# Fourier mixing and a gated FFN: the complex product summed on GpSimd, one inverse pass in place of two

## The chip, the cores and the metric

The kernel runs on one core of one Trainium2 chip. Its time is the device time of one execution in microseconds (us). Three runs of the kernel before took 885.06, 885.45 and 886.32 us, so the median is 885.45 us. The profile and the trace come from one further execution, which took 884.74 us.

A core has five engines, each with its own queue of instructions that it works through in order: TensorE (PE in the profile, with weight loads as PEld), VectorE (DVE), ScalarE (ACT), GpSimd (POOL) and SyncE (SP, which here only starts transfers). GpSimd starts transfers too. Engines wait for each other by semaphores. TensorE writes into PSUM, which has eight banks of 128 x 512 float32. ScalarE and VectorE read PSUM; in this kernel GpSimd works on SBUF alone.

## What is computed

```python
X = np.fft.rfft(x, axis=1)                       # x: (8, 3008, 256) float32
Y = X * (filt_r + 1j * filt_i)[None, :, :]       # filters: (1505, 256)
y = np.fft.irfft(Y, n=3008, axis=1)              # back to (8, 3008, 256)
t = y.reshape(24064, 256)
out = (np.maximum(t @ w_gate, 0.0) * (t @ w_val)) @ w_out   # widths 256 -> 1536 -> 256
```

The first three lines mix along the sequence of each of the 8 batches; the rest is a feed-forward part over all 24,064 tokens.

## The kernel before, in words

The sequence of 3008 is split as 94 x 32, and the transforms are done as matrix products. For each batch b there are five stages:

- A, the forward transform over 94. For batches 2 to 7 its input is loaded by `load_chunk` in four chunks j (six transfers each, started by GpSimd), folded by `fold_chunk` (six float32 additions and subtractions on GpSimd, L346 to L351), multiplied on TensorE in `tiled_a` (psF, L360), and stored to a buffer in device memory. `hold_gpsimd` (L259) puts a tiny copy on GpSimd in front of each load that waits for the newest `prod`, so that the load isn't started too early.
- `fwd(b, i)` for i = 0 to 5: the forward transform over 32, 16 matmuls of 64 x 32 weights into two banks psX (L396). The two halves r = 0 and 1 of the free dimension are the real and the imaginary part. The steps call it for two i at a time.
- `product(b, i, e, k)`: VectorE multiplies psX (both parts) by the real filter Ftr (k = 0, tile `tt`) or by the imaginary filter Fti (k = 1, tile `uu`), and writes bf16 (L413). `tt` and `uu` have four buffers each.
- `inv(b, q)` for q = 0 to 2: the inverse over 32. For each of two i and of two parts r there are two passes, k = 0 with the weights I2t over `tt`, and k = 1 with I2u over `uu`, and all four add up in PSUM: 64 matmuls of 32 x 64 weights and 256 columns into four banks psD (L428). I2u is I2t with its parts exchanged and signs changed, which does the complex arithmetic. ScalarE copies the four banks to `dsb` (L436), and SP stores it to device memory; `load_d` reads it back in another order.
- C, `item_c(k, h)`: the inverse over 94 for one block of 512 tokens (psY, L488), copied to `yT`, half h = 0 by ScalarE (L494) and half h = 1 by VectorE (L496).

The feed-forward part is the loop that everything else is hung into. The 24,064 tokens are 47 blocks k of 512, and each block has 12 steps. A step calls `gv` (four matmuls of 512 columns into psV and psG, a copy `vsb` on ScalarE, and on VectorE the `prod` of the gate and the value) and `o_part` of the block before (four matmuls of 256 columns into psO). After these two, the step calls the functions that were registered for it by `at_step`, in the order in which they were registered, and in steps 8 and 10 of a block `item_c` for the next block. There is no scheduler: this order is the order of every engine's queue. So a stage of a batch is put on TensorE by naming the global step, `k * 12 + ft`, at which it is called.

The steps are counted from `end`, a little before the batch's first output block. It is 51 for batch 1, and 123, 195, 267, 339, 411 and 483 for batches 2 to 7, 72 steps apart.

```python
l = (6, 14, 22, 30)[j] if b == 2 else end - 115 + NFT * j           # load of chunk j, then fold of chunk j - 1
l = (-37, -25, -13)[z] if b == 1 else -44 + 14 * z                  # start of fwd for pair z
at_step(end + l + (9 if b == 1 else 10) - (z == 2), lambda b=b, z=z: inv(b, z))
```

From `end + l` on, each of the 8 steps has one `product` (4 for the first i, 4 for the second), and `inv` follows behind them. The next batch's loads and folds are registered at steps of the present batch, for example those of batch 2 at steps 6 to 30, beside batch 1's products. In the prologue batch 0 runs alone, with 8 of its products on GpSimd (L411); it is not part of what is changed, except that its tables are shared.

Of the kernel before, what the change touches and what calls it, by code (L numbers as in the profile page):

```python
# [12 lines left out]
FP32 = mybir.dt.float32  # L13
BF16 = mybir.dt.bfloat16
ALU = mybir.AluOpType
# [16 lines left out]
NG = 24  # L32
# [3 lines left out]
def _ap(t, offset_elems, ap_list):  # L36
    return dataclasses.replace(
        t, offset=t.offset + offset_elems, ap=[list(p) for p in ap_list]
    )
# [77 lines left out]
def kernel(  # L117
# [10 lines left out]
    nc = tc.nc  # L128
    B, S_, D = x.shape
    DFF = moe_w_gate.shape[1]  # L130
    NFT = DFF // 128
# [11 lines left out]
    consts = ctx.enter_context(tc.tile_pool(name="consts", bufs=1))  # L143
# [5 lines left out]
    def bank(name, *shape):  # L149

        i = free.pop(0)
        t = ps.tile([128, *shape], FP32, tag=f"bank{i}", bufs=1, name=name)
        held[id(t)] = i, t
        return t

    def done(t):
        free.append(held.pop(id(t))[0])

    prologue = ExitStack()
    pro = prologue.enter_context(tc.tile_pool(name="pro", bufs=1))  # L160
# [12 lines left out]
    M1 = consts.tile([128, 2, N1], BF16)  # L173
    F2 = consts.tile([128, NG, 64], BF16)
    I2t = consts.tile([128, 2, NG // 2, 64], BF16)
    I2u = consts.tile([128, 2, NG // 2, 64], BF16)
    Ftr = consts.tile([128, NG // 2, D], BF16)
    Fti = consts.tile([128, NG // 2, D], BF16)
    WgT = consts.tile([128, 2, DFF], BF16)
# [17 lines left out]
    perm, conj, own = tabs[:, 0:64], tabs[:, 64:66], tabs[96:, 66:578]  # L197
# [94 lines left out]
    def turn_a(dst, src):  # L292

        nc.vector.transpose(dst.bitcast(FP32).rearrange("p k d -> p d k"),
                            src.bitcast(FP32).rearrange("p n d -> p d n"))
# [5 lines left out]
    def turn_1(i):  # L301
        w = D // 8
        src = AS1[1 + i // 2].rearrange("p l c d -> p (l c) d")
        turn_a(ats[1][:, 1, :, i * w:i * w + w], src[:, :, i % 2 * w:i % 2 * w + w])
# [36 lines left out]
    def fold_chunk(b, j):  # L341

        xp = XP[j]
        t = fs.tile([128, 2, 512], FP32, tag="fold", bufs=1, name="fold")
        tt = nc.gpsimd.tensor_tensor
        tt(t, xp[:, 0:2], xp[:, 2:4], op=ALU.add)  # L346
        tt(xp[:, 2:4], xp[:, 0:2], xp[:, 2:4], op=ALU.subtract)  # L347
        tt(xp[:, 1], xp[:, 2], xp[:, 3], op=ALU.add)
        tt(xp[:, 2], xp[:, 2], xp[:, 3], op=ALU.subtract)
        tt(xp[:, 0], t[:, 0], t[:, 1], op=ALU.add)  # L350
        tt(xp[:, 3], t[:, 0], t[:, 1], op=ALU.subtract)  # L351
        fold[b, j] = (xp[:, 0], xp[:, 3], xp[:, 1], xp[:, 2])

    def tiled_a(b, j):

        banks = [bank("psF", 2, D) for _ in range(4)]
        for c in range(4):
            for q in range(4):
                r = 32 * q
                nc.tensor.matmul(banks[q][32 * c:32 * c + 32], WF[r:r + 24, c, :],  # L360
                                 fold[b, j][c][r:r + 24], start=True, stop=True,
                                 tile_position=(r, 32 * c))
        asf = sb.tile([128, NC2 * D], BF16, tag="asb", bufs=3, name="asb")
        asf = asf.rearrange("p (n q d) -> p n q d", n=2, d=D)
        for q in range(4):
            copy = nc.scalar.copy if q % 2 == 0 else nc.vector.tensor_copy
            copy(asf[:, :, q, :], banks[q])  # L367
            done(banks[q])
        for c in range(4):
            nc.sync.dma_start(_ap(Abuf[b], ((48 * (c % 2) + 24 * (1 - c // 2)) * N2 + 8 * j) * D,  # L370
                                  [[N2 * D, 24], [1, 8 * D]]),
                              asf[32 * c:32 * c + 24])
# [12 lines left out]
    psXs, tus, left = {}, {}, {}  # L385
# [15 lines left out]
    def product(b, i, e, k, pool=False):  # L401

        psX = psXs[b, i, e]
        pool_, bufs = (fs, 4) if b else (pro, 8)
        p = pool_.tile([128, 2, D], BF16, tag=("tt", "uu")[k], bufs=bufs, name=("tt", "uu")[k])
        filt = (Ftr, Fti)[k][:, 2 * i + e, :]
        filt = dataclasses.replace(filt, ap=[list(filt.ap[0]), [0, 2], list(filt.ap[1])])
        if pool:
            xs = pro.tile([128, 2, D], FP32, tag="xs", bufs=3)
            nc.scalar.copy(xs, psX)  # L410
            nc.gpsimd.tensor_tensor(p, xs, filt, op=ALU.mult)  # L411
        else:
            nc.vector.tensor_tensor(p, psX, filt, op=ALU.mult)  # L413
        tus[b, i, e, k] = p
        left[b, i, e] -= 1
        if not left[b, i, e]:
            done(psX)

    def inv(b, q):

        psD = [bank("psD", 2, D) for c in range(4)]
        for m in range(2):
            for k in range(2):
                for r in range(2):
                    for c in range(4):
                        for e in range(2):
                            i = 2 * q + m
                            nc.tensor.matmul(psD[c][64 * e:64 * e + 64, m],  # L428
                                             (I2t, I2u)[k][32 * c:32 * c + 32, r, 2 * i + e, :],
                                             tus[b, i, e, k][32 * c:32 * c + 32, r],  # L430
                                             start=(k == r == 0), stop=(k == r == 1),
                                             tile_position=(32 * c, 64 * e))
        dst = sb.tile([128, 8, D], BF16, tag="dsb", bufs=3, name="dsb") if b else DS0[:, 8 * q:8 * q + 8, :]
        for c in range(4):
            copy = nc.vector.tensor_copy if not b and q == 2 and c < 2 else nc.scalar.copy
            copy(dst[:, c:8:4, :], psD[c])  # L436
            done(psD[c])
        if b:
            for z in range(4):
                nc.sync.dma_start(_ap(Dbuf[b], (64 * (z // 2) + z % 2) * NG * D + 8 * q * D,  # L440
                                      [[2 * NG * D, 32], [1, 8 * D]]),
                                  dst[32 * z:32 * z + 32])

    def first_b(amid):

# [36 lines left out]
    def item_c(k, h):  # L482

        if h == 0:
            yTs[k] = sb.tile([128, 2, W], BF16, tag="yT", bufs=3, name="yT")
        psY = bank("psY", W)
        for (o, b, n2, n1, w) in runs(k * W, W):
            nc.tensor.matmul(psY[:, o:o + w],  # L488
                             dCs[b, n2 // 8][:, n2 % 8, h * 128:(h + 1) * 128],
                             M1[:, 1, n1:n1 + w] if b == 0 else M1[:NROW, 0, n1:n1 + w],  # L490
                             start=True, stop=True)
        dst = yTs[k][:, h]
        if h == 0:
            nc.scalar.copy(dst, psY)  # L494
        else:
            nc.vector.tensor_copy(dst, psY)  # L496
        done(psY)
# [66 lines left out]
    q = NX2 * D // 4  # L564
# [54 lines left out]
    for p, s, h in items:  # L619
# [4 lines left out]
        if (p, s, h) == (3, 0, 1):  # L624
            for hh in range(2):
                item_c(0, hh)
    turn_1(0)
    nc.sync.dma_start(WF, nc.inline_tensor(fold_h, name="dft_fold").ap())
    prologue.close()
    fs = ctx.enter_context(tc.tile_pool(name="fs", bufs=2))  # L630
# [3 lines left out]
    def at_step(s, f):  # L634
        side.setdefault(s, []).append(f)
# [3 lines left out]
        at_step((4, 9, 12)[k - 1], lambda k=k: turn_1(k))  # L639
    for b in range(1, B):  # L640
        end = (b * S // W - 1) * NFT + C_AT[0] - 5
        if b > 1:
            for j, e in enumerate((-72, -67, -62, -57)):
                l = (6, 14, 22, 30)[j] if b == 2 else end - 115 + NFT * j

                def next_x(b=b, j=j, l=l):
                    hold_gpsimd(prods[-1][:, 0:8])
                    load_chunk(b, j)
                    if j:
                        fold_chunk(b, j - 1)  # L650
                    if j == 3:
                        fold_chunk(b, j)
                at_step(l, next_x)
                at_step(end + e, lambda b=b, j=j: tiled_a(b, j))
            at_step(end + e + 4, lambda b=b: load_at_tiled(b))
        for z in range(3):
            l = (-37, -25, -13)[z] if b == 1 else -44 + 14 * z
            for i in (2 * z, 2 * z + 1):
                at_step(end + l, lambda b=b, i=i: fwd(b, i))
                for h in range(4):  # L660
                    at_step(end + l + i % 2 * 4 + h, lambda b=b, i=i, h=h: product(b, i, h // 2, h % 2))
            at_step(end + l + (9 if b == 1 else 10) - (z == 2), lambda b=b, z=z: inv(b, z))
        at_step(end - 2, lambda b=b: load_d(b))
    prev = None
    for k in range(NB):
# [40 lines left out]
```

## Time and profile before

| | before |
|---|---|
| device time, median of 3 runs | 885.45 us |
| the profiled execution: device time | 884.74 us |
| the profiled execution: span of the instructions | 883.0 us |
| busy share PE / DVE / ACT / POOL | 98% / 65% / 56% / 41% |
| granted TensorE clock, mean | 1.00 |
| 564 copies `vsb` (ACT) | 592 ns each |
| 564 `prod` (DVE) | 690 ns each |
| products of L413 (DVE), 128x512 to bf16 | 681 to 683 ns each |
| 1536 matmuls of psD | 264 to 293 ns each, up to 8 of them at work side by side |
| GpSimd's additions, 128x1024 / 128x512 float32 | 2349 to 2358 / 1267 to 1269 ns each |

The span runs from the first instruction to the last; 1.74 us of the device time lie outside it. A duration of a matmul in the profile is from its start to its modelled end, and matmuls overlap, so their rate is read from the distance between starts. Durations of GpSimd are rough too, and the distance between starts is the surer reading there.

### The profile page before, as it was taken

The numbers are of one execution on the slowest core, as the hardware profiler recorded it, in microseconds if no ns is written. First come the engines' busy times: TensorE is split into PE (matmuls) and PEld (weight loads), VectorE is DVE, ScalarE is ACT, GpSimd is POOL, SyncE is SP. The second block draws the span as 40 slices with busy tenths as digits, with TensorE's granted clock in tenths as the row PEclk, the third lists the DMA queues.
The fourth block names the chain that finished last, engine by engine and source line by source line (L and its number), as shares of the span: only waits on it lengthen the run. The fifth ranks groups of instructions, "written<-read, shape, count | busy, mean of one in ns | idle before, by whom it ended". The sixth has DMA issues, their size and how long they took to land.

```text
span 883.0 us, 21560 instructions
## 1 busy us (share of the span) xinstructions
PE 869.7 (98%) x8381; PEld 508.5 (58%) x8381; DVE 577.4 (65%) x864; ACT 493.6 (56%) x899; POOL 365.7 (41%) x374
## 2 busy tenths in 40 slices
PE   8899999999999999999999999999999999999998
PEld 4345655566556565556555655556655656566665
DVE  3777766776567666667765676657766677555553
ACT  4665555555655565555555555555555555554553
POOL 7818940166901688016970278603794000000001
PEclk9999999999999999999999999999999999999999
DMA  9694453633745447543466344664445512511111
GB/s 238 179 190 110 127 139 102 135 93 102 198 98 105 111 118 177 111 106 104 134 154 129 102 112 124 153 126 110 109 144 123 118 52 58 122 35 36 37 31 54
DMA packets 104192, 101.69 MB, mean 115 GB/s; under 512 B 24235, under 2 KB 92363, under 8 KB 103322
## 3 DMA queue, kind: packets, MB, share of 16 engines
q1 hardware_dynamic: 80954, 73.10, 34.1%
q0 software_dynamic: 22736, 26.42, 12.4%
q8 instruction: 66, 1.08, 0.5%
q10 hardware_dynamic: 400, 0.79, 0.3%
q14 instruction: 36, 0.29, 0.1%
HBM read 58.23 MB, written 45.88 MB: 118 GB/s over the span
## 4 chain that ended last, share of the span: by engine, by line
PE 92%; DMA 3%; DVE 2%; ACT 2%; issue 1%; POOL 1%; ACTq 0%; DVEq 0%
PE psV L505 28%; PE psO L526 27%; PE psG L505 27%; PE psF L360 3%; PE psD L428 3%; PE psY L488 2%; PE psA L267 1%; PE psX L396 1%; DMA Fti<-in_filt_i_dram 1%; ACT dsb L436 1%; DMA XF<-in_x_dram 1%; DMA Ftr<-in_filt_r_dram 1%; DVE yT L496 1%; DVE tt L413 0%; DVE prod L510 0%
## 5 line engine op out<-in xcount | busy, mean ns | idle before, releaser
L510 DVE SCALAR_TENSOR_TENSOR prod<-psG,vsb 128x512 bf16<-128x512 f32 x564 | 386.1, 690 | 257.4 <-ACT vsb L508 251.2
L508 ACT CAST vsb<-psV 128x512 bf16<-128x512 f32 x564 | 330.3, 592 | 265.6 <-PE psV L505 158.6
L505 PE MATMUL psV<-yT,WvT 128*128 128x512 bf16 x1128 | 338.6, 379 | 2.9 <-DVE yT L496 2.9
L526 PE MATMUL psO<-WoT,prod 128*128 128x256 bf16 x2256 | 336.5, 273 | 0.0
L505 PE MATMUL psG<-yT,WgT 128*128 128x512 bf16 x1128 | 335.3, 379 | 0.0
L526 PEld LDWEIGHTS <-prod 128*128 128x128 bf16 x2256 | 220.7, 98 | 143.4
L505 PEld LDWEIGHTS <-WgT 128*128 128x128 bf16 x1128 | 110.0, 97 | 139.1 <-issue 7.8
L259 POOL CAST scr<-prod 128x8 f32<-128x8 bf16 x24 | 4.6, 190 | 290.3 <-DVE prod L510 274.9
L505 PEld LDWEIGHTS <-WvT 128*128 128x128 bf16 x1128 | 99.9, 98 | 34.5 <-issue 22.9
L550 POOL DMA_DIRECT2D out_dram<-osb x5 | 2.6, 536 | 201.8 <-ACT osb L539 201.8
L539 ACT COPY osb<-psO 128x512 f32<-128x512 f32 x92 | 53.9, 586 | 25.8 <-PE psO L526 25.0
L413 DVE TENSOR_TENSOR tt<-psX,Ftr 128x512 bf16<-128x512 f32 x96 | 65.1, 683 | 3.2 <-PE psX L396 1.7
L413 DVE TENSOR_TENSOR uu<-psX,Fti 128x512 bf16<-128x512 f32 x88 | 59.9, 681 | 0.0
L333 POOL DMA_DIRECT2D XF<-in_x_dram x96 | 56.7, 596 | 3.2 <-PE psG L505 1.5
L347 POOL TENSOR_TENSOR XF<-XF 128x1024 f32<-128x1024 f32 x24 | 56.4, 2349 | 1.9
L346 POOL TENSOR_TENSOR fold<-XF 128x1024 f32<-128x1024 f32 x24 | 56.6, 2358 | 0.8
L436 ACT CAST dsb<-psD 128x512 bf16<-128x512 f32 x84 | 43.1, 600 | 19.9 <-PE psD L428 19.9
L367 ACT CAST asb<-psF 128x512 bf16<-128x512 f32 x48 | 25.8, 589 | 34.6 <-PE psF L360 34.6
L367 DVE CAST asb<-psF 128x512 bf16<-128x512 f32 x48 | 30.9, 686 | 17.9 <-PE psF L360 17.2
L488 PEld LDWEIGHTS <-dCb 96*128 96x128 bf16 (+1 forms) x604 | 33.5, 97 | 9.2 <-issue 7.0
L488 PE MATMUL psY<-M,dCb 96*128 96x94 bf16 (+19 forms) x604 | 37.6, 199 | 0.0
L494 ACT CAST yT<-psY 128x512 bf16<-128x512 f32 x47 | 28.3, 602 | 14.2 <-PE psY L488 14.1
(64 smaller groups left out, 456.6 us busy)
## 6 DMA issues: line engine op xcount, KB each, us to landing
XF<-in_x_dram POOLq DMA_DIRECT2D x48, 256.0 KB, 6.3
Dbuf<-dsb SPq DMA_DIRECT2D x84, 128.0 KB
dCb<-Dbuf SPq DMA_DIRECT2D x56, 192.0 KB
XF<-in_x_dram POOLq DMA_DIRECT2D x96, 96.0 KB, 2.7
Abuf<-asb SPq DMA_DIRECT2D x96, 96.0 KB
at<-Abuf SPq DMA_DIRECT2D x24, 384.0 KB
out_dram<-osb SPq DMA_DIRECT2D x69, 94.0 KB
XF<-in_x_dram SPq DMA_DIRECT2D x20, 256.0 KB
```

The lines of the kernel that those rows point to most:

```text
L333: nc.gpsimd.dma_start(xp[r:r + 24, 0:4:2, :], _ap(x, (b * N1 * N2 + o) * D, [[N2 * D, 24], [47 * N2 * D, 2], [1, 512]]))
L346: tt(t, xp[:, 0:2], xp[:, 2:4], op=ALU.add)
L347: tt(xp[:, 2:4], xp[:, 0:2], xp[:, 2:4], op=ALU.subtract)
L367: copy(asf[:, :, q, :], banks[q])
L413: nc.vector.tensor_tensor(p, psX, filt, op=ALU.mult)
L436: copy(dst[:, c:8:4, :], psD[c])
L488: nc.tensor.matmul(psY[:, o:o + w], dCs[b, n2 // 8][:, n2 % 8, h * 128:(h + 1) * 128], M1[:, 1, n1:n1 + w] if b == 0 else M1[:NROW, 0, n1: ...
L505: nc.tensor.matmul(pt[:, :W], w[:, h, ft * 128:(ft + 1) * 128], yt[:, h, :], start=(h == 0), stop=(h == 1))
L508: nc.scalar.copy(vsb, psV[:, :W])
L510: nc.vector.scalar_tensor_tensor(prod, in0=psG[:, :W], scalar=0.0, in1=vsb, op0=ALU.max, op1=ALU.mult)
L526: nc.tensor.matmul(psO[:, t % 2], prods[ft][:, t * 128:(t + 1) * 128], WoT[:, ft, :], start=(ft == 0), stop=(ft == NFT - 1))
L539: copy(osb[:, t0 % 2:t % 2 + 1], psO[:, t0 % 2:t % 2 + 1])
```

## The change

- **One inverse pass.** For batches 1 to 7, VectorE writes `tt` and `uu` in float32, with three buffers each instead of four. A new function `add` has GpSimd form `pp`, bf16, with six buffers: `tt` of the real part minus `uu` of the imaginary part, and `tt` of the imaginary part plus `uu` of the real part, two instructions of 128 x 256 for each i and e. `inv` then has one pass over `pp` with I2t: 32 matmuls instead of 64. The signs that I2u carried go into Fti, which GpSimd multiplies once by a column of signs at the end of the prologue. Batch 0 keeps its two passes.
- **Inverse copies.** Banks 1 and 3 of psD are copied by VectorE, banks 0 and 2 by ScalarE, and the second two, with the store, come one step later.
- **C's copies.** From block 5 on, both halves of `yT` are copied by ScalarE.
- **Starts.** Pairs start at `end` - 38, -26, -14 for batch 1 (one step earlier each), and at `end` - 44, -31, -18 for the others (the second one step, the third two steps earlier). `inv` comes 10 steps behind the start everywhere.
- **Loads and folds.** A chunk's fold is registered at a step of its own. For batch 2 the loads stay at 6, 14, 22, 30 and the folds are at 11, 23, 35, 47. For batch b above 2 the loads are at `end` - 130 + 14 j, and the folds, counted from the `end` of batch b - 1, at -52, -35, -22 and -9.

```diff
-    I2u = consts.tile([128, 2, NG // 2, 64], BF16)
+    I2u = pro.tile([128, 2, NG // 2, 64], BF16)
...
-        pool_, bufs = (fs, 4) if b else (pro, 8)
-        p = pool_.tile([128, 2, D], BF16, tag=("tt", "uu")[k], bufs=bufs, name=("tt", "uu")[k])
+        pool_, bufs, dt = (fs, 3, FP32) if b else (pro, 8, BF16)
+        p = pool_.tile([128, 2, D], dt, tag=("tt", "uu")[k], bufs=bufs, name=("tt", "uu")[k])
...
+    def add(b, i, e):
+
+        tt, uu = (tus.pop((b, i, e, k)) for k in range(2))
+        p = tus[b, i, e, 0] = fs.tile([128, 2, D], BF16, tag="pp", bufs=6, name="pp")
+        nc.gpsimd.tensor_tensor(p[:, 0], tt[:, 0], uu[:, 1], op=ALU.subtract)
+        nc.gpsimd.tensor_tensor(p[:, 1], tt[:, 1], uu[:, 0], op=ALU.add)
+
     def inv(b, q):
 
         psD = [bank("psD", 2, D) for c in range(4)]
+        last = 0 if b else 1
         for m in range(2):
-            for k in range(2):
+            for k in range(last + 1):
...
-                                             start=(k == r == 0), stop=(k == r == 1),
+                                             start=(k == r == 0), stop=(k == last and r == 1),
...
-        for c in range(4):
-            copy = nc.vector.tensor_copy if not b and q == 2 and c < 2 else nc.scalar.copy
-            copy(dst[:, c:8:4, :], psD[c])
-            done(psD[c])
-        if b:
+        def out(cs):
+            for c in cs:
+                copy = nc.vector.tensor_copy if (c % 2 if b else q == 2 and c < 2) else nc.scalar.copy
+                copy(dst[:, c:8:4, :], psD[c])
+                done(psD[c])
+        if not b:
+            return out(range(4))
+
+        def rest():
+            out((2, 3))
             for z in range(4):
                 nc.sync.dma_start(_ap(Dbuf[b], (64 * (z // 2) + z % 2) * NG * D + 8 * q * D,
                                       [[2 * NG * D, 32], [1, 8 * D]]),
                                   dst[32 * z:32 * z + 32])
+        out((0, 1))
+        return rest
...
-        if h == 0:
+        if h == 0 or k > 4:
             nc.scalar.copy(dst, psY)
...
+    nc.gpsimd.tensor_scalar(Fti, Fti, conj[:, 0:1], 1.0, op0=ALU.mult, op1=ALU.mult)
...
+        starts = [(-38, -26, -14), (-44, -31, -18)][b > 1]
         if b > 1:
             for j, e in enumerate((-72, -67, -62, -57)):
-                l = (6, 14, 22, 30)[j] if b == 2 else end - 115 + NFT * j
-
-                def next_x(b=b, j=j, l=l):
+                l = (6, 14, 22, 30)[j] if b == 2 else end - 130 + 14 * j
+                fold_at = ((11, 23, 35, 47)[j] if b == 2 else
+                           end - 72 + ((-52,) + tuple(v + 9 for v in (-44, -31, -18)))[j])
+
+                def next_x(b=b, j=j):
                     hold_gpsimd(prods[-1][:, 0:8])
                     load_chunk(b, j)
-                    if j:
-                        fold_chunk(b, j - 1)
-                    if j == 3:
-                        fold_chunk(b, j)
                 at_step(l, next_x)
+                at_step(fold_at, lambda b=b, j=j: fold_chunk(b, j))
...
-        for z in range(3):
-            l = (-37, -25, -13)[z] if b == 1 else -44 + 14 * z
+        for z, l in enumerate(starts):
             for i in (2 * z, 2 * z + 1):
                 at_step(end + l, lambda b=b, i=i: fwd(b, i))
                 for h in range(4):
                     at_step(end + l + i % 2 * 4 + h, lambda b=b, i=i, h=h: product(b, i, h // 2, h % 2))
-            at_step(end + l + (9 if b == 1 else 10) - (z == 2), lambda b=b, z=z: inv(b, z))
+                    if h % 2:
+                        at_step(end + l + i % 2 * 4 + h, lambda b=b, i=i, h=h: add(b, i, h // 2))
+
+            def back(b=b, z=z, s=end + l + 10):
+                at_step(s + 1, inv(b, z))
+            at_step(end + l + 10, back)
```

## The prediction, made before the changed kernel was run

> **What bounds the kernel now.** I read the page's table of engines first, then the chain that ended last in order of time, then GpSimd's timeline in batch 1, because the change puts work on GpSimd.
>
> ```profile
> PE 869.7 (98%) x8381; PEld 508.5 (58%) x8381; DVE 577.4 (65%) x864; ACT 493.6 (56%) x899; POOL 365.7 (41%) x374
> ```
>
> TensorE is the bound; every other engine has a third of its time or more free. From the chain (start, us, what):
>
> ```profile
> 79.98 0.44 PE psO L526 x4
> 80.42 1.01 PE psD L428 x64
> ...
> 85.44 0.56 PE psX L396 x32
> ...
> 98.26 1.01 PE psD L428 x64
> ```
>
> ```profile
> 540.67 1.05 PE psD L428 x64
> ...
> 544.80 0.57 issue
> 545.37 0.41 DVE prod L510
> 545.78 0.19 issue
> 545.97 0.69 DVE yT L496
> ```
>
> An inverse takes TensorE 1.01 us; 32 matmuls of the same kind of packing (psX) take 0.56. The second stretch is the only kind of place in the steady part where TensorE isn't itself the chain: behind a batch's third inverse, ScalarE's four copies delay VectorE, and `yT` comes late. A step without additions is 1.30 us of TensorE (psV 0.43, psG 0.43, psO 0.44). GpSimd's timeline while batch 1 is transformed (start, us, what):
>
> ```profile
> 59.51 0.19 POOL L259 CAST scr<-prod 128x8 f32<-128x8 bf16 x1 [15.36 <-issue]
> 60.21 2.39 POOL L333 DMA_DIRECT2D XF<-in_x_dram  x4 [0.51 <-DMA at<-Abuf]
> 62.57 1.40 POOL L337 DMA_DIRECT2D XF<-in_x_dram  x2
> ...
> 72.48 2.35 POOL L346 TENSOR_TENSOR fold<-XF 128x1024 f32<-128x1024 f32 x1
> 74.92 2.34 POOL L347 TENSOR_TENSOR XF<-XF 128x1024 f32<-128x1024 f32 x1
> 77.34 1.27 POOL L348 TENSOR_TENSOR XF<-XF 128x512 f32<-128x512 f32 x1
> 78.68 1.27 POOL L349 TENSOR_TENSOR XF<-XF 128x512 f32<-128x512 f32 x1
> 79.91 1.27 POOL L350 TENSOR_TENSOR XF<-fold 128x512 f32<-128x512 f32 x1
> 81.13 1.28 POOL L351 TENSOR_TENSOR XF<-fold 128x512 f32<-128x512 f32 x1
> 82.35 0.20 POOL L259 CAST scr<-prod 128x8 f32<-128x8 bf16 x1
> 82.48 2.36 POOL L333 DMA_DIRECT2D XF<-in_x_dram  x4
> 84.83 1.40 POOL L337 DMA_DIRECT2D XF<-in_x_dram  x2
> 86.25 2.36 POOL L346 TENSOR_TENSOR fold<-XF 128x1024 f32<-128x1024 f32 x1
> ```
>
> A fold holds GpSimd for 9.87 us (72.48 to 82.35), a load with its hold for 3.90 us (82.35 to 86.25), and between 72 and 120 us it hardly pauses. No other engine waits for any of this until `tiled_a`. That freedom is what the change spends.
>
> **What is removed.** Seven batches have three inverses each. Each goes from 1.01 us to the 0.56 us of psX's 32 matmuls: 21 x 0.45 = 9.45 us off TensorE, which is the bound, so all of it counts. The late `yT` goes too: comparing the distance between the starts of psV and psG at the first step of every block with the usual 0.43 us, I find 18 late blocks from block 7 on, 0.11 to 0.51 us each, 4.4 us together. With half 1 copied by ScalarE at 0.60 us, and only two of the four inverse copies there, the copy is ready in time: psY ends 1.55 us into its step, waiting some 0.2 us and the copy bring it to 2.35, and the next block starts at 2.85. I take 4.4; the ends are 0 and 4.4. Gains: 13.85 us.
>
> **What is added at no cost.** VectorE's products write float32. The nearest rows are ScalarE's: 128x512 to float32 586 ns, to bf16 592. VectorE is still the same 0.68 per product. VectorE gives up 42 copies of `yT` and takes 42 of psD at the same 0.68 us; ScalarE the reverse at 0.60. The sign multiplication of Fti is 128x3072 on GpSimd; 128x768 took 0.90 us, so about 3.6, between 44 and 60 us, where GpSimd waits 15.36 us. If that cover were gone it would delay the first load by as much. SP's queue gets the same four stores, one step later; the read-back is five steps behind them in the steady batches and one in batch 1, whose C starts seven steps later.
>
> **What is added on GpSimd.** Each pair of `add` is two instructions of 128 x 256. Independent 128x512 additions start 1.23 us apart, 128x1024 ones 2.44; dependent 128x512 ones 1.34. The slope is 1.10 us per 512, so 128x256 takes 1.23 - 0.55 = 0.68, a pair 1.36. The bounds: the bf16 product of L411 (1.12 apart, 128x512) gives 0.6, the recorded durations 0.73, so 1.2 to 1.46. I take 1.36, from the rows with the same float32 inputs. 84 pairs are 114 us on an engine that was 41% busy. The total has room; the order is the question. Each pair waits for its `uu`, the fourth product of an i waits for the first pair to give back its `tt` buffer (three buffers), and the inverse waits for all four pairs. Whatever stands ahead of a pair in GpSimd's queue now delays TensorE.
>
> **Batch 1.** GpSimd's queue from the calls: load 0 (step 6), fold 0 (step 11), pair 1 (step 14), load 1 (14), pairs 2 to 4, load 2 (22), fold 1 (23), pairs 1 to 3 of the second inverse, load 3 (30), pair 4, fold 2 (35). Load 0's last transfer starts at 63.27; these transfers landed 5.1 to 9.5 us after issue, and the last packet of this one ended at 68.4. Fold 0 starts at 68.5 and ends at 78.4. Pair 1, though its `uu` is there by 69.3, ends at 79.7; load 1 83.6; pairs 2 to 4 87.7. The first inverse stays at step 23, that is 80.42 by the chain; its second half, 0.28 later, needs all pairs. Wait: 87.7 - 80.7 = 7.0 us. Then load 2 to 91.6, fold 1 to 101.5, three pairs to 105.6, load 3 to 109.5, pair 4 to 110.9. The second inverse stays at step 35: 98.26 - 0.45 + 0.28 = 98.1. So TensorE is 12.8 us late in all, whichever way it is split between standing at the inverse and standing earlier, when VectorE is blocked at the fourth `tt` with the `prod` behind it. The third inverse (step 47, about 128.0) finds its pairs done at 126.2. With a pair at 1.2 or 1.46 us the 12.8 becomes 11.5 to 13.6; a landing 1 us later adds 1. I take 12.8.
>
> **Batches 2 to 6.** Take batch 5. Pairs of the first inverse end at 499.4 (the last `uu` ends at 498.1 in the trace), 1.2 us before it is due. Fold 1 to 509.2, pair 1, load 2 and three pairs to 518.6; the second inverse needs them at 519.7. Fold 2 must wait for load 2, whose last transfer starts at 513.8 and lands 5.9 us later (median of the window around this batch's load at 506.7): 519.7. It ends at 529.6; pair 1 530.9, load 3 534.8, three pairs 538.9. The third inverse's second half is due at 538.5 (540.67, one step of 1.30 and 0.90 of shorter inverses earlier, 0.25 of `yT` waits less, 0.28 on). Wait 0.4 us, times five batches: 2.0. Ends: none with a landing of 5.1, and 0.8 each at the overall median of 6.3, so 0 to 4.2. Batch 7 has no loads behind it and no wait.
>
> **Sum.** 883.0 - 9.45 - 4.4 + 12.8 + 2.0 = 883.95 us of span, 885.7 us with the 1.74 us around it, against 884.74 for the profiled execution. That execution is 0.71 us under the median, so I forecast 885.45 + 0.95 = **886.4 us**: the gain is spent within batch 1.
>
> **Rivals.**
> - TensorE's clock falls while it stands. At the start of the trace the first 18 matmuls of 256 columns are 213 ns apart, where psO's are 109: half pace until about 5 us, after idleness. In batch 1 I get one stand of 4.4 us at the second inverse; the longest in the trace of before is about 1.4 us, with no half pace after it. If half pace for 3.7 us follows, as at the start, it costs 1.9 us: 888.3. [...] No run here shows a stand of that length.
> - Loads land late. At 7.5 us instead of 5.9 (inside the 5.1 to 9.5 seen) each steady third inverse waits 2.0 us, 10 in all instead of 2: 894.4; half of that excess gives 890.
> - The other side: GpSimd's small additions cost less than the line through the larger ones. The place is the chain of eight pairs in batch 1. At 0.8 us a pair the batch loses 8.3 us and the steady batches nothing: -13.85 + 8.3, so 879.9. The sign turns at about 1.2 us a pair. For it: L411's bf16 row is 9% under the float32 one, and spans on GpSimd are rough. Against it: the starts of 24 folds repeat to 0.1 us, and the two folds in batch 1's chain, 20 us, stay whatever a pair costs. With every wait gone it would be 871.6.
>
> **Chances.** Forecast 0.50 (its own range 883.5 to 889), clock 0.14, late loads 0.14, cheap pairs 0.22. Three runs of this kernel differ by 0.14%, so 0.2%, 1.8 us, is about what can be told from no change: slower means above 887.2, faster below 883.7. Of the forecast's 0.50 I put 0.34 within, 0.14 above, 0.02 below. That makes slower 0.42, same 0.34, faster 0.24. The range 882 to 892 leaves out most of the cheap pairs and the worst of the late loads, about 0.18.
>
> **What would show it.** psD's groups of 32 at 0.56 us; no wait of psV for `yT` from block 7 on; in the waits, psD held up by GpSimd's `pp`, most of it twice in batch 1 near 80 and 100 us, and VectorE's `tt` held up by `pp` just before; folds back to back with pairs there. The forecast is wrong if psD doesn't wait in batch 1, if pairs start much nearer than 1.36 us, or if third inverses wait for more than a microsecond.

## The result, and the profile after

| | before | changed |
|---|---|---|
| median device time | 885.88 us (885.06 to 886.35, 4 runs) | 928.0 us (925.67 to 930.61, 4 runs) |
| ratio | 1 | 1.0477, 95% interval 1.0446 to 1.0508 |
| span of the profiled execution | 883.0 us | 923.9 us |
| granted TensorE clock, mean | 1.00 | 0.982 |

The changed kernel is 4.8% slower; 886.4 us was forecast, with a range up to 892. The page's tables of engines and of the 40 slices:

```profile
PE 879.5 (95%) x7709; PEld 506.6 (55%) x7709; DVE 584.7 (63%) x864; ACT 496.2 (54%) x899; POOL 484.2 (52%) x543
...
PEclk9998999999999999999999999999999999999999
```

TensorE has 672 matmuls fewer and is busy longer; its clock was below full pace now and then (0.982 in the mean), which a slice shows only once. The waits (who waited for whom: us, times, longest):

```profile
PE psD L436 <- POOL pp L423: 11.7, 13, 3.3
...
PE psX L396 <- DMA at<-Abuf: 7.9, 3, 3.5
DVE tt L413 <- POOL pp L424: 7.0, 4, 4.9
...
PE psX L396 <- DMA out_dram<-osb: 5.3, 2, 3.4
```

psD waits for `pp`, as the forecast had it. But psX, the first `fwd` of a batch, waits as well, for the read of `at`, and the forecast has nothing on that. (Where this view names the store of `osb`, another transfer that ended last is named for the same kind of wait.) One such place on TensorE's timeline, batch 5:

```profile
518.74 0.63 PE L396 MATMUL psX<-at,F 64*32 64x256 bf16 x31 [3.45 <-DMA at<-Abuf]
519.30 1.03 PE L520 MATMUL psV<-yT,WvT 128*128 128x512 bf16 x2
520.12 1.06 PE L520 MATMUL psG<-yT,WgT 128*128 128x512 bf16 x2
520.98 1.06 PE L541 MATMUL psO<-WoT,prod 128*128 128x256 bf16 x4
521.83 0.63 PE L503 MATMUL psY<-M,dCb 96*128 96x78 bf16 x6
```

The starts behind the wait are 0.82 to 0.86 us apart where they were 0.43: half pace, for about 3 us. The trace has the granted clock as well. The same place in stretches of 3.41 us (the stretch, its length, TensorE's busy time and matmuls, the granted clock, the share of the DMA engines and GB/s):

```profile
512.48:515.89 3.41, 2.81 (x17) 1.00 1.20 190
515.89:519.30 3.41, 0.56 (x32) 1.00 0.67 136
519.30:522.71 3.41, 3.41 (x23) 0.50 0.59 154
522.71:526.13 3.42, 3.42 (x26) 1.00 0.61 163
```

So it is the clock, and it is halved for exactly one such stretch. I read the whole trace by the distance between the starts of TensorE's groups and what is usual for the same group, and sorted the excess (sums are of unrounded values):

| difference of the spans, us | batch or place | us |
|---|---|---|
| first `fwd` waits for `at` | 2, 3, 4, 5, 6 | 2.0, 3.0, 2.1, 3.7, 4.0 = 14.9 |
| third inverse waits for `pp` | 2, 3, 4, 5, 6 | 2.6, 2.3, 3.3, 2.4, 3.4 = 13.9 |
| waits of batch 1 for GpSimd | steps 22, 23, 35 | 3.1, 3.1, 4.2 = 10.4 |
| half pace behind a wait | 8 places | 14.1 |
| shorter inverses, late `yT` gone | everywhere | -13.9 |
| not sorted | | 1.5 |
| sum | | 40.9 |

GpSimd in batch 1 of the changed kernel (start, us, what):

```profile
69.36 2.35 POOL L346 TENSOR_TENSOR fold<-XF 128x1024 f32<-128x1024 f32 x1 [5.50 <-DMA XF<-in_x_dram]
...
79.25 0.72 POOL L423 TENSOR_TENSOR pp<-tt,uu 128x256 bf16<-128x256 f32 x1
...
87.28 0.71 POOL L423 TENSOR_TENSOR pp<-tt,uu 128x256 bf16<-128x256 f32 x1
87.96 0.71 POOL L424 TENSOR_TENSOR pp<-tt,uu 128x256 bf16<-128x256 f32 x1
...
111.22 0.73 POOL L424 TENSOR_TENSOR pp<-tt,uu 128x256 bf16<-128x256 f32 x1
```

and VectorE at the same time:

```profile
80.68 0.69 DVE L413 TENSOR_TENSOR tt<-psX,Ftr 128x512 f32<-128x512 f32 x1 [4.92 <-POOL pp L424]
```

Fold 0 holds the first pair until 79.25. The pairs of the first inverse are done at 88.7 (87.7 was forecast), those of the second at 111.95 (110.9), and between, VectorE stands 4.9 us at the fourth `tt`. The two instructions of a pair start 0.68 us apart, as estimated.

### The profile page after: what moved, and what is told of

It reads as the page before. It is cut to its first block, busy times and chain, and to the rows that moved or that the text cites. A ratio compares the mean times of both kernels' runs of the same rounds, so it can differ in the third digit from the quotient of the medians.

```text
span 923.9 us, 20546 instructions
## 1 busy us (share of the span) xinstructions
PE 879.5 (95%) x7709; PEld 506.6 (55%) x7709; DVE 584.7 (63%) x864; ACT 496.2 (54%) x899; POOL 484.2 (52%) x543
## 4 chain that ended last, share of the span: by engine, by line
PE 61%; POOL 16%; DMA 15%; issue 3%; DVE 2%; ACT 1%; SPq 1%; POOLq 0%; ACTq 0%; DVEq 0%
PE psV L520 18%; PE psO L541 18%; PE psG L520 17%; DMA XF<-in_x_dram 6%; DMA at<-Abuf 6%; PE psF L360 3%; POOL XF L333 3%; DMA Abuf<-asb 2%; POOL pp L423 2%; POOL pp L424 2%; POOL XF L347 2%; POOL fold L346 2%; PE psY L503 2%; PE psA L267 2%; POOL XF L348 1%
## 5 line engine op out<-in xcount | busy, mean ns | idle before, releaser
L541 PE MATMUL psO<-WoT,prod 128*128 128x256 bf16 x2256 | 341.4, 275 | 0.0
L520 PE MATMUL psG<-yT,WgT 128*128 128x512 bf16 x1128 | 340.0, 383 | 0.0
L423 POOL TENSOR_TENSOR pp<-tt,uu 128x256 bf16<-128x256 f32 x84 | 61.0, 726 | 98.4 <-PE psG L520 58.0
L413 DVE TENSOR_TENSOR tt<-psX,Ftr 128x512 f32<-128x512 f32 (+1 forms) x96 | 65.3, 684 | 25.2 <-PE psX L396 16.4
L509 ACT CAST yT<-psY 128x512 bf16<-128x512 f32 x89 | 52.2, 587 | 48.3 <-PE psY L503 48.2
L424 POOL TENSOR_TENSOR pp<-tt,uu 128x256 bf16<-128x256 f32 x84 | 60.8, 724 | 0.0
L413 DVE TENSOR_TENSOR uu<-psX,Fti 128x512 f32<-128x512 f32 (+1 forms) x88 | 59.9, 681 | 0.0
L445 DVE CAST dsb<-psD 128x512 bf16<-128x512 f32 x42 | 28.8, 686 | 24.7 <-PE psD L436 23.9
```

The source lines that it names most:

```text
L423: nc.gpsimd.tensor_tensor(p[:, 0], tt[:, 0], uu[:, 1], op=ALU.subtract)
L424: nc.gpsimd.tensor_tensor(p[:, 1], tt[:, 1], uu[:, 0], op=ALU.add)
L520: nc.tensor.matmul(pt[:, :W], w[:, h, ft * 128:(ft + 1) * 128], yt[:, h, :], start=(h == 0), stop=(h == 1))
L541: nc.tensor.matmul(psO[:, t % 2], prods[ft][:, t * 128:(t + 1) * 128], WoT[:, ft, :], start=(ft == 0), stop=(ft == NFT - 1))
```

## The experiments

Two theories of the wait at `fwd` stood against each other after the result. **A**: it is a matter of transfers. The load of the next batch's chunk 0 moved from 115 to 130 steps ahead of `end`, and there it falls just ahead of the last store of the folded first stage, which `load_at_tiled` must read back. **B**: GpSimd's fuller queue or the earlier steps make the read late.

**Two parts of the change alone.** First the copies of `yT`, in the kernel before:

```diff
-        if h == 0:
+        if h == 0 or k > 4:
             nc.scalar.copy(dst, psY)
```

> The kernel before with one part of the change: from block 5 on, both halves of yT are copied by ScalarE. Theory: the 18 late starts of a block (0.11 to 0.51 us each) go, 4.4 us, so about 881.5 us. Rival: ScalarE, with all four inverse copies still its own, passes the lateness on, and the time stays at 885.9 us.

Measured: 880.43 us against 884.88, ratio 0.9956 (0.9941 to 0.9971). The theory holds: 4.45 us by the medians where 4.4 were worked out, so ScalarE with four inverse copies passes no lateness on that shows.

Then the one pass, also in the kernel before (the imaginary filter is left out of its output):

```diff
+        last = 0 if b else 1
         for m in range(2):
-            for k in range(2):
+            for k in range(last + 1):
...
-                                             start=(k == r == 0), stop=(k == r == 1),
+                                             start=(k == r == 0), stop=(k == last and r == 1),
```

> The kernel before with the second pass of the inverse (I2u over uu) left out for batches 1 to 7; uu is still made and not used, so the imaginary filter is missing from the output. Theory: TensorE is the bound and loses 21 x 0.45 us, 9.45 in all, about 876.4 us. Rival: part of it is taken back at ScalarE's four copies behind each inverse, and less than 6 us are gained.

Measured: 875.62 us against 884.88, ratio 0.9896 (0.9881 to 0.9911), 9.3 us. The chain of that run:

```profile
515.46 0.57 PE psD L429 x32
534.17 0.61 PE psD L429 x32
```

Together the two are worth 13.7 us: the forecast's gains are there.

**One move of a load alone.** The kernel before, with chunk 0 loaded where the change has it:

```diff
-                l = (6, 14, 22, 30)[j] if b == 2 else end - 115 + NFT * j
+                l = (6, 14, 22, 30)[j] if b == 2 else end - 115 + NFT * j - (0 if j else 15)
```

> The kernel before with one move of the change: for batches 3 to 7 the load of chunk 0 is registered 15 steps earlier, where the change has it; no pairs on GpSimd, all else as before. Theory A (transfers): the load falls between the last store of the folded first stage and the read that brings it back, delays that read, and the first fwd of batches 2 to 6 waits 2 to 4 us each, some with TensorE at half pace behind them: 12 to 20 us slower, 898 to 906 us. Theory B (GpSimd's queue is the cause of the wait at fwd): nothing changes, 885.9 us.

Measured: 904.19 us against 884.88, ratio 1.0219 (1.0202 to 1.0236). 19.3 us slower without a single pair on GpSimd: theory B falls as the main cause. SP's queue, batch 5: the last store of the first stage (Abuf<-asb) and the read that waits for it (at<-Abuf), first in the kernel before, then in the kernel with the one move:

```profile
470.61 1.53 SPq L370 DMA_DIRECT2D Abuf<-asb  x4
473.86 2.91 SPq L378 DMA_DIRECT2D at<-Abuf  x4
```

```profile
479.93 1.96 SPq L370 DMA_DIRECT2D Abuf<-asb  x4
487.82 2.72 SPq L378 DMA_DIRECT2D at<-Abuf  x4
```

The read starts 3.25 us behind the store in the one and 7.89 us in the other. The load was started from GpSimd at 476.80, 3.1 us ahead of the store. The changed kernel has 8.66 us here (499.08 and 507.74).

The other batches don't all look like batch 5. From the store's start to the read's start, for batches 2, 3, 4 and 6, it is 3.60, 3.73, 4.60 and 4.94 us in the kernel before, 7.03, 4.58, 7.60 and 8.95 with the one move, and 7.25, 4.93, 7.54 and 8.88 in the changed kernel. In batch 3 only the first of the read's four transfers starts nearly on time; all four take 6.98 us (with the move) and 6.40 us (changed) to be issued, against 2.90 before.

**The same move undone in the changed kernel**, not by putting it back, but eight steps earlier still, so that it has landed before the store:

```diff
-                l = (6, 14, 22, 30)[j] if b == 2 else end - 130 + 14 * j
+                l = (6, 14, 22, 30)[j] if b == 2 else end - 130 + 14 * j - (0 if j else 8)
```

> The changed kernel with the load of chunk 0 of batches 3 to 7 eight steps earlier, well ahead of the last store; folds unmoved. Theory A: the five waits at the first fwd (14.9 us) and the half pace behind three of them (4.5 us) go: about 908.6 us. Theory B: the read is late for another reason, and the time stays near 928 us.

Measured: 906.74 us, 1.0258 (1.0227 to 1.0288) of before. The waits at `fwd` are gone but for 0.15 us once, and the read starts 2.97 us behind the store again:

```profile
490.88 1.52 SPq L370 DMA_DIRECT2D Abuf<-asb  x4
493.85 2.87 SPq L378 DMA_DIRECT2D at<-Abuf  x4
```

So the load's place is both enough to cause the wait (in the kernel before) and what has to go to end it (in the changed one).

**The third inverse.**

```diff
-                l = (6, 14, 22, 30)[j] if b == 2 else end - 130 + 14 * j
+                l = (6, 14, 22, 30)[j] if b == 2 else end - 130 + 14 * j + (6 if j == 3 else 0)
                 fold_at = ((11, 23, 35, 47)[j] if b == 2 else
-                           end - 72 + ((-52,) + tuple(v + 9 for v in (-44, -31, -18)))[j])
+                           end - 72 + (-52, -35, -22, -2)[j])
```

> The changed kernel with the load of chunk 3 of batches 3 to 7 six steps later, behind the pairs of the third inverse in GpSimd's queue, and its fold seven steps later. Theory: the 3.90 us of that load stand ahead of pairs 2 to 4 and are what makes five third inverses wait 2.3 to 3.4 us (13.9 in all, and 4.9 of half pace behind three of them); all of it goes: about 909 us. Rival: fold 2, late because its load lands late, is the cause by itself; then the third inverses go on waiting and the time stays above 920 us.

Measured: 908.09 us, 1.0253 (1.0222 to 1.0284) of before; no third inverse waits. GpSimd behind batch 5's second inverse, with the changed kernel's first line of the same stretch ahead of it:

```profile
555.30 2.35 POOL L346 TENSOR_TENSOR fold<-XF 128x1024 f32<-128x1024 f32 x1 [2.77 <-DMA XF<-in_x_dram]
```

```profile
544.77 2.35 POOL L346 TENSOR_TENSOR fold<-XF 128x1024 f32<-128x1024 f32 x1 [2.77 <-DMA XF<-in_x_dram]
...
554.65 0.72 POOL L423 TENSOR_TENSOR pp<-tt,uu 128x256 bf16<-128x256 f32 x1
...
559.56 0.72 POOL L424 TENSOR_TENSOR pp<-tt,uu 128x256 bf16<-128x256 f32 x1
```

Fold 2 still waits 2.77 us for its load, and the last pair is still done at 560.3, 1.2 us before psD's first matmul at 561.5. So the late landing of load 2 alone doesn't make the inverse wait. In the changed kernel the 3.9 us of load 3 stood in the same chain. Put back in front of the pairs, they would have them done at 564.2 here, 2.4 us after the inverse's second half is due (561.8, 0.28 us behind its first matmul), and 2.4 us is the wait in the changed kernel. The lateness of load 2 taken away instead, 1.7 us, would leave an estimated 0.7 us; that was not run.

**Batch 1.**

```diff
-                l = (6, 14, 22, 30)[j] if b == 2 else end - 130 + 14 * j
-                fold_at = ((11, 23, 35, 47)[j] if b == 2 else
+                l = (6, 9, 12, 44)[j] if b == 2 else end - 130 + 14 * j
+                fold_at = ((21, 33, 45, 46)[j] if b == 2 else
```

> The changed kernel with batch 2's loads registered at steps 6, 9, 12, 44 and its folds at 21, 33, 45, 46, so that the pairs of batch 1 have no fold ahead of them in GpSimd's queue when they become ready. Theory: the two waits in batch 1 (10.4 us, at TensorE's eighth step behind the start and at the two inverses) and the half pace behind them (4.7 us) go: about 913 us. Rival: the loads, now bunched, delay the first batch's own transfers, and less than half of it is gained, above 920 us.

Measured: 910.53 us, 1.0274 (1.0251 to 1.0296) of before. All waits of batch 1 behind its first `fwd` are gone, 17.5 us by the medians where 15.1 were worked out. What was not foreseen: the third of the bunched loads waited on GpSimd, by the trace for transfers of the earlier ones, 1.37 us before its first transfer and 1.67 us before its second:

```profile
70.85 1.78 POOL L333 DMA_DIRECT2D XF<-in_x_dram  x3 [1.67 <-DMA XF<-in_x_dram]
```

The pairs behind it were done at 80.2 all the same, just in time for the inverse.

**All three moves** in the changed kernel:

```diff
-                l = (6, 14, 22, 30)[j] if b == 2 else end - 130 + 14 * j
-                fold_at = ((11, 23, 35, 47)[j] if b == 2 else
-                           end - 72 + ((-52,) + tuple(v + 9 for v in (-44, -31, -18)))[j])
+                l = (6, 9, 12, 44)[j] if b == 2 else (end - 138, end - 116, end - 102, end - 82)[j]
+                fold_at = ((21, 33, 45, 46)[j] if b == 2 else
+                           end - 72 + (-52, -35, -22, -2)[j])
```

> The changed kernel with all three moves of loads and folds: chunk 0 early, chunk 3 late, batch 2's around batch 1's pairs. Theory: what is left is the gain on TensorE, 9.45 us of shorter inverses and 4.4 us of late yT: 13.9 us under the kernel before, about 871.5 us. Rival: the waits only move on to the next transfer or fold, and the time stays above 880 us.

Measured: 872.37 us (871.18 to 872.6) against 885.53, ratio 0.984 (0.9818 to 0.9863). This version beats both kernels: it is 13.2 us under before by the medians, 1.6%, and the interval leaves out 1. GpSimd is busy for as long as in the changed kernel, and TensorE is the chain again:

```profile
PE 850.6 (98%) x7587; PEld 499.0 (57%) x7709; DVE 584.0 (67%) x864; ACT 495.3 (57%) x899; POOL 484.7 (56%) x543
...
PE 91%; DVE 3%; DMA 2%; ACT 2%; issue 1%; POOL 1%; SPq 0%; DVEq 0%; ACTq 0%
```

(122 of its matmul records are missing from the trace, so its busy time reads a little low.)

**Half pace.** Is it the standing that halves the pace, or are the operands late?

```diff
+    def fill(n):
+
+        psJ = bank("psJ", 512)
+        for i in range(n):
+            nc.tensor.matmul(psJ, WvT[:, 0, 0:128], WvT[:, 1, 0:512], start=True, stop=True)
+        done(psJ)
...
+        if b > 1:
+            at_step(end + starts[0], lambda: fill(9))
         for z, l in enumerate(starts):
```

> The changed kernel with nine matmuls of 512 columns, whose result is not used, put on TensorE ahead of the first fwd of batches 2 to 7; the waits for the read stay as they are, but TensorE stands 1.9 us less in each. Theory (clock): half pace follows only stands of about 2.5 us and more, so it disappears behind the first fwd of the three batches that had it, 4.5 us; batch 7, where little was waited for, loses up to 1.9: about 925 us. Rival (the slow matmuls behind a wait have another cause, such as late operands): half pace stays, and the time is 928 to 930 us.

Measured: 924.28 us (921.61 to 930.84), 1.044 (1.0391 to 1.0488) of before. The interval overlaps the changed kernel's, so the time decides nothing. The trace does. The same place in batch 5:

```profile
517.33 2.11 PE L391 MATMUL psJ<-WvT 128*128 128x512 bf16 x9
519.36 0.28 PE L403 MATMUL psX<-at,F 64*32 64x256 bf16 x1
521.02 0.63 PE L403 MATMUL psX<-at,F 64*32 64x256 bf16 x31 [1.38 <-DMA out_dram<-osb]
521.58 0.61 PE L527 MATMUL psV<-yT,WvT 128*128 128x512 bf16 x2
522.02 0.38 PE L527 MATMUL psG<-yT,WgT 128*128 128x512 bf16 x1
```

The read is as late as before, the stand is 1.66 us instead of 3.7, and what is behind it starts 0.44 us apart. No first `fwd` of this kernel is followed by half pace, while its inverses in batches 1, 2, 3, 4 and 6 still are. The operands are as late as before, so they are not what halves the pace.

It is not simply the length of the stand either. In the traces that have halved stretches (the changed kernel, e3 to e6 and e8, with mean clocks of 0.982 to 0.994), the clock changed only at points of one grid, 3.41 us apart: in the changed kernel the nine halved stretches start at 82.39, 89.22, 113.11, 236.00, 294.02, 461.27, 519.30, 631.94 and 689.97 us, whole multiples of 3.413 us from each other. The stretches just ahead of these nine hold 0.22 to 1.88 us of matmuls. In e8 the stand in batch 5 lies across a point of the grid, its two stretches hold 2.77 and 2.62 us, and no half clock followed:

```profile
516.87:520.28 3.41, 2.77 (x15) 1.00 1.06 179
520.28:523.69 3.41, 2.62 (x47) 1.00 0.50 145
```

In the six traces with such stands, from 75 us to 10 us before the end, every stretch at full clock with less than 1.6 us of matmuls was followed by half clock, none with more than 2.2 us was, and in between both occurred (in the changed kernel 1.85 and 1.88 us were followed by it, 1.67, 1.70, 1.96 and 2.15 us were not).

## Why the prediction was wrong

**What is removed** held: 9.45 us for the shorter inverses (9.3 measured by itself) and 4.4 for the late `yT` (4.4 by the medians).

**What is added at no cost** held for the engines: the float32 products take 681 to 684 ns, as the bf16 ones did, the signs took 2.9 us where 3.6 were estimated, and e7 shows no new wait of TensorE for copies, signs or stores.

**What is added on GpSimd** held: 0.68 us per instruction of 128 x 256.

**Batch 1** held in its mechanism and nearly in its size: the queue's order was worked out within 1.1 us, and the wait came in the two forms named. 12.8 us of lateness were forecast. The trace shows 10.4 us of standing and 4.7 us of half pace, which is lateness too.

**Batches 2 to 6** is the first step that failed, in the size of a term. The wait of the third inverse was put at 0.4 us from a landing 5.9 us behind the last transfer's start. In batch 5 the last transfer started at 547.7 and the fold at 555.3, 7.6 us, and 7.6 to 8.6 us in the five batches; the median over all loads in the profile's list of transfers rose from 6.3 to 7.3. The chain as worked out, with load 3 in it, had no slack, so the 1.7 us went straight into it: 2.3 to 3.4 us in each batch instead of 0.4. The rival of late loads had this mechanism and, at 7.5 us, gave 2.0 us per batch; it was given 0.14.

**The step that is missing altogether** is the transfer of load 0. In the change part by part, a load was priced by the 3.90 us that it holds GpSimd's queue, and never by what its 0.92 MB do to other transfers in the stretch that it was moved to. There it delayed the store's landing, in batch 5 by 5.4 us (8.66 against 3.25 to the read's start), and behind that store stand the read, the first `fwd` and TensorE: 14.9 us of waits, 19 to 21 us with the half pace (e3, e4). The read had little to spare: before the change psX starts 12.7 us behind the read's start in batch 5 and 10.9 in batch 6, and where TensorE waits in the changed kernel, in batches 2, 4, 5 and 6, it goes on 10.4 to 11.0 us behind it. The chain view of before doesn't show that, because a wait that is just met leaves no line.

**The clock** was given a chance of 0.14, one occasion and 1.9 us. It came at 8 places, 1.2 to 3.0 us each, 14.1 in all (batch 1's first place, with two stands and two halved stretches, is the 3.0). The one stand of 4.4 us that the rival allows for is not worked out: by the sum above it, 12.8 less 7.0 leaves 5.8 us for the second inverse; 4.2 were measured. The 7.0 us at the first inverse, which the rival leaves out, became two stands of 3.1 us, and each was followed by half pace. The trace of the changed kernel shows the clock halved for 3.41 us at a time, on a grid, behind stretches that still hold 0.56 us (batch 5, first `fwd`) and 1.88 us (batch 6, third inverse) of matmuls, and behind a stand as short as 2.6 us (batch 2, third inverse, 1.59 us of matmuls in the stretch ahead). At the start of the trace, where the rival read half pace from the distance between starts, the granted clock of before is 1.00 (1 to 5 us); that the clock slowed the matmuls there is not shown.

**The rival on the other side**, cheaper pairs, fell: pairs cost what the line through the larger additions gave.

Between the span that was forecast, 883.95 us, and the 923.9 us measured lie 40.0 us: 14.9 from the transfer of load 0, 11.9 from the third inverses (13.9 instead of 2.0), 14.1 from the clock and 1.5 not sorted, less 2.4 because batch 1 stood 10.4 instead of 12.8. The range left out the first altogether and priced the clock for one wait; there were thirteen waits and nine halved stretches.

## What to carry to other kernels

When a transfer is moved, follow it twice: through the queue of the engine that starts it, and through the transfers that are in flight where it now falls, above all a store that is read straight back (in batch 5 the read started 8.66 us behind the store where it had been 3.25). In the changed kernel 39.2 us of stands on TensorE, 2.0 to 4.2 us each, brought 14.1 us of half pace on top, so here a place on a queue that is free of what becomes ready late was worth more than the engine's busy share says. Moving an operation to an engine that is half idle (GpSimd, 41% busy before) was a question of order here: the same 84 pairs cost 4.8% or gave 1.6%, by where four loads and four folds stand around them.

## What the runs showed of the hardware that was not expected

- A load of 0.92 MB started from GpSimd 3.1 to 3.3 us ahead of a store from SP's queue (changed kernel, batches 2 to 6) made the read behind the store start 7.0 to 9.0 us after the store's start in four of five batches (e3 and the changed kernel), against 3.3 to 4.9 in the kernel before, though the store itself was issued in 1.5 to 3.5 us.
- Half clock on TensorE came in stretches of 3.41 us on one grid, behind a stretch in which it had worked for 2.2 us or less (each time when it was below 1.6 us). The length of a stand alone did not tell whether it came: in the changed kernel stands of 2.0, 2.1, 2.3 and 2.4 us were not followed by it and those of 2.6 to 4.2 us were, but one of 2.2 us (e8, batch 2) was, and one of 3.6 us (e6, batch 4, an inverse that waits in several pieces) was not; it lies across a point of the grid, with 2.48 and 1.91 us of matmuls in the two stretches.
- Load 2 lands 7.6 to 8.6 us behind its last start in the changed kernel, where the load in the nearest stretch of before took 5.9. Why is open; it was not tried.
